# Q and K transposed by the DMA for six of eight batches, with a new order of attention work, loads and early matmuls, in a fused attention and feed-forward kernel

## Chip, cores, metric

One core of a Trainium2 chip. The metric is device time in microseconds (us). One execution of each kernel was also profiled; its span, from first to last instruction, is 1.7 to 1.8 us shorter than the time of that same execution. TensorE is called warm here where its granted clock is full, and cold where it is half.

## The reference, cut

```python
# q, k, v: (8 batches, 12 heads, 448 rows, 64), float32
scores = (1 / sqrt(64)) * q @ k.T
attn   = maximum(scores, 0) ** 2 / 448
x      = (attn @ v), heads side by side          # (3584, 768)
xn     = x / sqrt(mean(x * x, -1) + 1e-6) * rms_g
out    = (silu(xn @ w_gate) * (xn @ w_val)) @ w_out   # d_ff = 1536
```

## The kernel before

All matmuls are bf16. Work is cut into units; for each batch b the units of the feed-forward of b ("main") are merged with the attention units of b+1 ("side"). Each engine runs its own instructions in the order in which the program emits them, so a unit's place decides what stands behind what on every engine.

```python
def head_rows(t, b, h0, h1):                       # 4 rows of a head stand next to each other: 512-byte pieces in bf16
    return t[b, h0:h1].rearrange("h (p c) d -> p h (c d)", c=NCH)      # p = 112, c = 4
...
for s in range(NSL):                               # weights in 4 slices
    load_w("g", s)
    load_w("v", s)
    if s == 1:                                     # Q and K of batch 1 in the middle of the weights
        alloc_ld(1); load("q", 1); load("k", 1)
load("v", 1)
...
def reorder(b, j):                                 # VectorE: bring the two heads of a pair side by side
    for nm in ("q", "k"):
        t = tpool.tile([PC, NCH, 2, D], BF16, ...)
        nc.vector.tensor_copy(out=t (h c reordered), in_=ld[nm, b][:, 2*j : 2*j+2, :])
        ldp[nm, b, j] = t

def transposes(b, j):
    ...                                            # reorder(b, 0) if j == 0; reorder(b, j+1)
    psT = ps_a.tile([P, 2, S], BF16)
    for ti, nm in enumerate(("q", "k")):
        for c in range(NCH):
            nc.tensor.transpose(out=psT[:, ti, c*PC:(c+1)*PC], in_=ldp[nm, b, j][:, c], identity=ident)
    nc.vector.tensor_copy(out=t, in_=psT)          # PSUM to SBUF

def scores(b, j, cs):                              # 2 score buffers in PSUM (psS)
    ...                                            # matmuls into psS, then per chunk:
    relu on ScalarE (every fourth on VectorE); square at once on VectorE

def attention(b):
    units = [transposes(b, 0)]
    for j in range(HP):                            # 6 pairs of heads
        units += [scores(b, j, (0, 1)), transposes(b, j+1), scores(b, j, (2, 3)), attend(b, j-1)]
    units += [attend(b, HP-1)]

def norm(b):                                       # ones-matmul for the sums, sqrt (ACT), then on VectorE:
    nc.vector.reciprocal(out=rstd, in_=rstd)       # 2.95 us
    for kt in range(KT):                           # 6 x 0.61 us
        nc.vector.scalar_tensor_tensor(out=xn[:, kt], in0=xTs[b][:, kt], scalar=g_sb[:, kt], in1=rstd, ...)
...
merge(ffn(b), attention(b+1) + [norm(b+1)], 0.0, 0.1)   # side units spread over the first 90% of the main work
```

## Time and profile before

| | us |
|---|---|
| timed before, median (four timed runs, 547.5 to 551.92) | 548.75 |
| span of the profiled run | 544.9 |
| head: start to first gate matmul of batch 0 | 51.6 |
| first batch (feed-forward 0 with attention 1) | 64.5 |
| next six batches together | 379.0 |
| tail (feed-forward 7 alone) | 49.9 |

The four stretches run from one "first gate matmul of a batch" to the next, read from the timeline of TensorE.

The summary page, with busy time per engine, the tenths of busy time in 40 equal slices, the granted TensorE clock in tenths, and the chain of waits that ended last:

```profile
span 544.9 us, 7394 instructions
...
PE 485.1 (89%) x3024; PEld 236.1 (43%) x3024; DVE 338.6 (62%) x586; ACT 252.3 (46%) x369; POOL 34.4 (6%) x45
...
PE   3774999879999799888999799987999899989996
...
PEclk9976999979999899999999999999999999999999
...
PE 73%; DVE 14%; ACT 8%; issue 2%; DMA 1%; POOL 0%; ACTq 0%; POOLq 0%
PE psV L260 20%; PE psG L260 20%; PE psO L286 14%; PE psAV L207 8%; PE psS L182 8%; DVE xn L249 5%; DVE rstd L246 4%; ACT r L197 4%; PE psT L163 3%; ACT L243 2%; DVE r L198 2%; DVE r L195 1%; ACT rstd L243 1%; DMA kb<-in_k_dram 1%; ACT xT L
```

TensorE (PE) is the limit, but 14% of the chain is VectorE (DVE): there PE stood still. The stretches of the table, with the busy time of each engine (instructions in brackets), the clock, the share of the DMA engines and GB/s:

```profile
core 0: us, PE busy (x) PEld busy (x) DVE busy (x) ACT busy (x) POOL busy (x), PEclk, DMA share, GB/s
0.00:51.59 51.59, 27.48 (x158) 13.25 (x159) 36.43 (x67) 23.38 (x28) 20.42 (x30) 0.85 1.25 179
51.59:116.04 64.45, 59.28 (x369) 28.25 (x367) 42.35 (x73) 29.57 (x44) 2.80 (x3) 0.95 0.73 115
116.04:495.03 378.99, 354.48 (x2263) 171.21 (x2261) 249.63 (x430) 187.34 (x275) 11.19 (x12) 0.99 0.25 44
495.03:544.90 49.87, 43.81 (x242) 23.38 (x239) 10.22 (x17) 12.02 (x22) 0.00 (x0) 1.00 0.14 40
```

In the head VectorE is busy 36 of 52 us and PE only 27; in the six batches PE is busy 354 of 379 us. Tile names below: qp and kp are the reordered Q and K, psT their transposes in PSUM and qkT the copy of them, psS the scores and r their relu, psAV attention times V, psSS the sums for norm, psG and psV the gate and value units, psO the output projection. What PE waited for (total us, times, longest):

```profile
PE psT L163 <- DVE qp L148: 29.6, 8, 7.6
PE psS L182 <- ACT r L197: 7.4, 11, 1.0
PE psS L182 <- DVE r L195: 7.4, 9, 1.1
PE psS L182 <- DVE qkT L169: 4.3, 2, 3.3
```

The largest is the first transposes of a batch, which wait for the reorder copy of Q (tile qp): 4.8 us at the very start, where the copy itself waits for its load, 7.6 at the end of the head, and 2.9 at each of six later boundaries. The timeline of PE and of VectorE at the second boundary (start, duration, instruction, idle before it):

```profile
107.09 5.37 PE L286 MATMUL psO<-wo_sb,hT 128*128 128x256 bf16 x36
115.32 0.56 PE L163 MATMUL psT<-ident,qp 112*128 112x112 bf16 x4 [2.86 <-DVE qp L148]
115.67 0.58 PE L163 MATMUL psT<-ident,kp 112*128 112x112 bf16 x4
116.04 2.45 PE L260 MATMUL psG<-xn,wg_sb 128*128 128x448 bf16 x6
```

```profile
108.41 2.95 DVE L246 RECIPROCAL rstd<-rstd 128x448 f32<-128x448 f32 x1 [1.55 <-ACT rstd L243]
111.40 3.66 DVE L249 SCALAR_TENSOR_TENSOR xn<-xT,g_sb,rstd 128x448 bf16<-128x448 bf16 x6
114.98 0.29 DVE L148 COPY qp<-qb 112x512 bf16<-112x512 bf16 x1
```

PE finishes its output projection at 112.46 and stands until 115.32, because the copy of 0.29 us was emitted after norm and stands behind the reciprocal and six xn. The first gate unit after it is at half clock (2.24 us from start to start where a warm unit takes 1.13).

### The profile page before, as it was taken

What the parts mean: (1) busy time and instruction counts of PE and PEld (TensorE: products, weight loads), DVE (VectorE), ACT (ScalarE), POOL (GpSimd) and SP (SyncE); (2) the same over time, 40 slices, a digit from 0 to 9 for tenths busy, and PEclk for the clock granted to TensorE, in tenths of its full rate; (3) what the DMA queues carried; (4) which work ended last, traced back from release to release, by engine and by line L of the source; (5) the groups of instructions that cost most, each with busy time, mean ns of one, the idle gap of its engine ahead of it and who ended that gap; (6) DMA issues with size and microseconds to landing.
All of it is one profiled execution on the core that took longest, in us unless ns stands there. A gap on an engine that the chain in (4) does not pass through costs nothing.

```text
span 544.9 us, 7394 instructions
## 1 busy us (share of the span) xinstructions
PE 485.1 (89%) x3024; PEld 236.1 (43%) x3024; DVE 338.6 (62%) x586; ACT 252.3 (46%) x369; POOL 34.4 (6%) x45
## 2 busy tenths in 40 slices
PE   3774999879999799888999799987999899989996
PEld 1331444434444344444444444444445444444553
DVE  3886677467764677566774677656775677745210
ACT  2553454524545354535444454454545445553221
POOL 7330001000010001000010000100000000000000
PEclk9976999979999899999999999999999999999999
DMA  9999938150073402560054500733001200002013
GB/s 114 201 201 205 203 53 102 35 103 1 1 102 73 95 1 24 79 123 16 1 75 86 108 1 1 103 58 80 1 1 29 78 10 2 1 29 59 0 30 88
DMA packets 45858, 35.08 MB, mean 64 GB/s; under 512 B 2304, under 2 KB 42240, under 8 KB 45824
## 3 DMA queue, kind: packets, MB, share of 16 engines
q0 software_dynamic: 40560, 23.60, 31.7%
q1 hardware_dynamic: 5264, 11.02, 6.8%
q8 instruction: 23, 0.38, 0.3%
q14 instruction: 11, 0.09, 0.1%
HBM read 47.19 MB, written 11.01 MB: 107 GB/s over the span
## 4 chain that ended last, share of the span: by engine, by line
PE 73%; DVE 14%; ACT 8%; issue 2%; DMA 1%; POOL 0%; ACTq 0%; POOLq 0%
PE psV L260 20%; PE psG L260 20%; PE psO L286 14%; PE psAV L207 8%; PE psS L182 8%; DVE xn L249 5%; DVE rstd L246 4%; ACT r L197 4%; PE psT L163 3%; ACT L243 2%; DVE r L198 2%; DVE r L195 1%; ACT rstd L243 1%; DMA kb<-in_k_dram 1%; ACT xT L215 1%
## 5 line engine op out<-in xcount | busy, mean ns | idle before, releaser
L198 DVE TENSOR_TENSOR r<-r 112x896 bf16<-112x896 bf16 x192 | 119.3, 625 | 93.8 <-ACT r L197 91.9
L197 ACT ACTIVATE r<-psS 112x896 bf16<-112x896 f32 x144 | 127.0, 916 | 52.5 <-PE psS L182 52.4
L260 PE MATMUL psG<-xn,wg_sb 128*128 128x448 bf16 x576 | 129.4, 360 | 1.1 <-DVE xn L249 1.0
L260 PE MATMUL psV<-xn,wv_sb 128*128 128x448 bf16 x576 | 128.0, 359 | 0.0
L286 PE MATMUL psO<-wo_sb,hT 128*128 128x512 bf16 (+1 forms) x672 | 115.2, 326 | 0.0
L271 ACT ACTIVATE sil<-psG 128x448 bf16<-128x448 f32 x96 | 52.3, 545 | 102.2 <-PE psG L260 90.8
L277 DVE TENSOR_TENSOR hT<-sil,psV 128x448 bf16<-128x448 bf16 x96 | 59.4, 618 | 45.9 <-PE psV L260 37.8
L286 PEld LDWEIGHTS <-hT 128*128 128x128 bf16 x672 | 63.6, 98 | 49.2 <-issue 9.3
L182 PE MATMUL psS<-qkT 64*112 64x448 bf16 x384 | 64.5, 394 | 19.3 <-ACT r L197 7.4
L260 PEld LDWEIGHTS <-wg_sb 128*128 128x128 bf16 x576 | 53.0, 99 | 59.8 <-issue 19.2
L260 PEld LDWEIGHTS <-wv_sb 128*128 128x128 bf16 x576 | 52.3, 99 | 57.5 <-issue 19.2
L293 ACT COPY ost<-psO 128x512 f32<-128x512 f32 (+1 forms) x56 | 26.9, 480 | 81.4 <-PE psO L286 81.4
L195 DVE TENSOR_SCALAR r<-psS 112x896 bf16<-112x896 f32 x48 | 52.0, 1084 | 0.0
L207 PE MATMUL psAV<-r,vb 112*64 112x448 bf16 x384 | 47.7, 370 | 4.6 <-DVE qkT L169 3.8
L182 PEld LDWEIGHTS <-qkT 64*112 64x112 bf16 x384 | 21.1, 131 | 60.5 <-issue 55.2
L163 PE MATMUL psT<-ident,qp 112*128 112x112 bf16 x192 | 19.0, 226 | 29.6 <-DVE qp L148 29.6
L215 ACT ACTIVATE xT<-psAV 128x448 bf16<-128x448 f32 x48 | 26.1, 545 | 33.7 <-PE psAV L207 33.7
L163 PEld LDWEIGHTS <-qp 112*128 112x128 bf16 x192 | 14.0, 103 | 40.9 <-DVE qp L148 31.9
L207 PEld LDWEIGHTS <-vb 112*64 112x64 bf16 x384 | 19.1, 111 | 28.9 <-issue 21.4
L246 DVE RECIPROCAL rstd<-rstd 128x448 f32<-128x448 f32 x8 | 23.6, 2953 | 12.8 <-ACT rstd L243 12.8
L169 DVE COPY qkT<-psT 128x896 bf16<-128x896 bf16 x48 | 29.8, 620 | 2.3 <-PE psT L163 2.1
L249 DVE SCALAR_TENSOR_TENSOR xn<-xT,g_sb,rstd 128x448 bf16<-128x448 bf16 x48 | 29.3, 680 | 0.3
(39 smaller groups left out, 157.6 us busy)
## 6 DMA issues: line engine op xcount, KB each, us to landing
qb<-in_q_dram POOLq DMA_DIRECT2D x7, 672.0 KB, 7.3
kb<-in_k_dram POOLq DMA_DIRECT2D x7, 672.0 KB, 9.8
vb<-in_v_dram POOLq DMA_DIRECT2D x7, 672.0 KB, 8.1
out_dram<-ost SPq DMA_DIRECT2D x8, 336.0 KB, 2.8
wg_sb<-in_moe_w_gate_dram POOLq DMA_DIRECT2D x4, 576.0 KB, 20.2
wv_sb<-in_moe_w_val_dram POOLq DMA_DIRECT2D x4, 576.0 KB, 21.8
wo_sb<-in_moe_w_out_dram POOLq DMA_DIRECT2D x2, 1152.0 KB, 28.3
out_dram<-ost SPq DMA_DIRECT2D x8, 288.0 KB, 5.3
```

Of the source, the lines that this page charges most:

```text
L163: nc.tensor.transpose(out=psT[:, ti, c * PC : (c + 1) * PC], in_=ldp[nm, b, j][:, c, :, :], identity=ident[:],)
L182: nc.tensor.matmul(out=psS[:, hh, :S], lhsT=t[prt, 1, c * PC : (c + 1) * PC], rhs=t[prt, 0, :], start=True, stop=True,)
L195: nc.vector.tensor_relu(out=r[:], in_=psS[:, :, :S])
L197: nc.scalar.activation(out=r[:], in_=psS[:, :, :S], func=ACT.Relu)
L198: nc.vector.tensor_tensor(out=r[:], in0=r[:], in1=r[:], op=ALU.mult)
L207: nc.tensor.matmul(out=psAV[hh * D : (hh + 1) * D, :], lhsT=ld["v", b][:, 2 * j + hh, c * D : (c + 1) * D], rhs=rsq[b, j, c][:, hh, :], st ...
L246: nc.vector.reciprocal(out=rstd[:], in_=rstd[:])
L249: nc.vector.scalar_tensor_tensor(out=xn[:, kt, :], in0=xTs[b][:, kt, :], scalar=g_sb[:, kt : kt + 1], in1=rstd[:], op0=ALU.mult, op1=ALU.mult,
L260: nc.tensor.matmul(out=ps[:], lhsT=w_sb[:, kt, fb * P : (fb + 1) * P], rhs=xns[b][:, kt, :], start=(kt == 0), stop=(kt == KT - 1),)
L271: nc.scalar.activation(out=s[:], in_=psG[:], func=ACT.Silu)
L277: nc.vector.tensor_tensor(out=hTs[b // 2][:, fb, o : o + S], in0=sil[b, fb][:], in1=psV[:], op=ALU.mult)
L286: nc.tensor.matmul(out=ps[:, :w], lhsT=hTs[i][:, fk, t * P : (t + 1) * P], rhs=wo_sb[:, fk, o : o + w], start=(fk == 0), stop=(fk == FT - 1),)
```

## The change

Its intent: take transposes off PE and VectorE; keep PE warm and busy at the start; give norm and its VectorE work more matmuls to hide behind. It
- loads Q and K of batches 2 to 7 so that a row of all heads lies in one partition (128-byte pieces instead of 512), and transposes them from SBUF to SBUF with eight DMA transposes per batch, issued by SyncE (SP);
- transposes batches 0 and 1 on PE straight from the loaded layout, one head at a time (16 half-width transposes per pair instead of 8), without reorder copies;
- loads all gate and value weights before Q, K and V of batch 1;
- runs 40 matmuls on zeros in the head;
- defers each square by one unit, joins the second score unit with attend (15 side units instead of 25), and spreads the side work over 85% of the main work instead of 90%;
- in passing, moves three relus of batch 0 from VectorE to ScalarE, gives x one buffer instead of two, and puts the transposes of PE in another PSUM pool.

```diff
+    def transpose_dma(b):
+        new_qkT(b)
+        for ti, nm in enumerate(("q", "k")):
+            for c in range(NCH):
+                nc.sync.dma_start_transpose(
+                    out=qkT[b][:, :, ti, c * PC : (c + 1) * PC], in_=ld[nm, b][:, c, :]
+                )
...
+            nc.gpsimd.dma_start(
+                out=t[:].rearrange("p c (h d) -> p c h d", d=D)[:, :, h0:h1, :],
+                in_=src.rearrange("h (p c) d -> p c h d", c=NCH),
+            )
...
     for s in range(NSL):
         load_w("g", s)
         load_w("v", s)
-        if s == 1:
-            alloc_ld(1)
-            load("q", 1)
-            load("k", 1)
-    load("v", 1)
+    for nm in ("q", "k", "v"):
+        load(nm, 1)
...
-    def reorder(b, j):
...
             for c in range(NCH):
-                nc.tensor.transpose(out=psT[:, ti, ...], in_=ldp[nm, b, j][:, c, :, :], ...)
+                for hh in range(2):
+                    nc.tensor.transpose(out=psT[hh * D : (hh + 1) * D, ti, ...],
+                                        in_=ld[nm, b][:, 2 * j + hh, c * D : (c + 1) * D], ...)
...
+        if b < PE_T:                                  # PE_T = 2
+            add(0.4, lambda: transposes(b, 0))
         for j in range(HP):
...
+            add(1.2, lambda j=j: scores(b, j, (2, 3)), lambda j=j: j and attend(b, j - 1))
...
+    keep_busy(16)
...
+            at = len(main) * 2 // 3
+            main[at:at] = [(0, lambda b=b: transpose_dma(b + 2))]
-        for fn in merge(ffn(b), side, 0.0, 0.1):
+        for fn in merge(main, side, 0.0, 0.15):
```

More of the change, by code (lines that the diff above doesn't have):

```diff
@@ L66 @@
     ldpool = ctx.enter_context(tc.tile_pool(name="ld", bufs=2))
-    tpool = ctx.enter_context(tc.tile_pool(name="tsb", bufs=2))
+    qtpool = ctx.enter_context(tc.tile_pool(name="qkT", bufs=2))
     apool = ctx.enter_context(tc.tile_pool(name="attn", bufs=10))
-    xpool = ctx.enter_context(tc.tile_pool(name="xT", bufs=2))
+    xpool = ctx.enter_context(tc.tile_pool(name="xT", bufs=1))
     npool = ctx.enter_context(tc.tile_pool(name="norm", bufs=2))
@@ L76, with new_qkT @@
     ps_m = ctx.enter_context(tc.tile_pool(name="ps_m", bufs=3, space=bass.MemoryType.PSUM))
-    def head_rows(t, b, h0, h1):
-        return t[b, h0:h1].rearrange("h (p c) d -> p h (c d)", c=NCH)
     ld = {}
-    def alloc_ld(b):
-        for nm in ("q", "k", "v"):
-            ld[nm, b] = ldpool.tile([PC, H, NCH * D], BF16, name=nm + "b", tag=nm + "b")
+    qkT = {}
+    src_of = {"q": q, "k": k, "v": v}
+    PE_T = 2
     def load(nm, b, h0=0, h1=H):
-        src = {"q": q, "k": k, "v": v}[nm]
-        nc.gpsimd.dma_start(out=ld[nm, b][:, h0:h1, :], in_=head_rows(src, b, h0, h1))
+        runs = nm == "v" or b < PE_T
+        if (nm, b) not in ld:
+            shape = [PC, H, NCH * D] if runs else [PC, NCH, H * D]
+            ld[nm, b] = ldpool.tile(shape, BF16, name=nm + "b", tag=nm + "b")
+        t = ld[nm, b]
+        src = src_of[nm][b, h0:h1]
+        if runs:
+            nc.gpsimd.dma_start(out=t[:, h0:h1, :], in_=src.rearrange("h (p c) d -> p h (c d)", c=NCH))
+        else:
+            nc.gpsimd.dma_start(
+                out=t[:].rearrange("p c (h d) -> p c h d", d=D)[:, :, h0:h1, :],
+                in_=src.rearrange("h (p c) d -> p c h d", c=NCH),
+            )
+    def new_qkT(b):
+        qkT[b] = qtpool.tile([P, HP, 2, S], BF16, name="qkT", tag="qkT")
+    def transpose_dma(b):
[5 more added lines that the diff above has]
+                )
     wg_sb = wpool.tile([P, KT, F], BF16, name="wg_sb", tag="wg")
@@ L110, in load_wo, with keep_busy @@
         )
-    alloc_ld(0)
+    ones_bf = const.tile([P, P], BF16, name="ones_bf", tag="ones_bf")
+    nc.vector.memset(ones_bf[:], 1.0)
+    busy_bf = const.tile([P, S], BF16, name="busy_bf", tag="busy_bf")
+    nc.vector.memset(busy_bf[:], 0.0)
+    def keep_busy(n):
+        ps = ps_m.tile([P, S], FP32, name="psB", tag="mm")
+        for _ in range(n):
+            nc.tensor.matmul(out=ps[:], lhsT=ones_bf[:], rhs=busy_bf[:], start=True, stop=True)
     load("q", 0, 0, 2)
@@ L116 @@
     masks.make_identity(nc, ident[:])
-    ones_bf = const.tile([P, P], BF16, name="ones_bf", tag="ones_bf")
-    nc.vector.memset(ones_bf[:], 1.0)
     eps_col = const.tile([P, 1], FP32, name="eps_col", tag="eps_col")
@@ L141, with relu_on, square_on, flush @@
     xTs = {}
-    qkT = {}
-    ldp = {}
-    def reorder(b, j):
-        for nm in ("q", "k"):
-            t = tpool.tile([PC, NCH, 2, D], BF16, name=nm + "p", tag=nm + "p")
-            nc.vector.tensor_copy(
-                out=t[:].rearrange("p c h d -> p h c d"),
-                in_=ld[nm, b][:, 2 * j : 2 * j + 2, :].rearrange("p h (c d) -> p h c d", c=NCH),
-            )
-            ldp[nm, b, j] = t
     def transposes(b, j):
         if j == 0:
-            xTs[b] = xpool.tile([P, KT, S], BF16, name="xT", tag="xT")
-            reorder(b, 0)
-        if j + 1 < HP:
-            reorder(b, j + 1)
-        psT = ps_a.tile([P, 2, S], BF16, name="psT", tag="ps_a")
+            new_qkT(b)
+        psT = ps_m.tile([P, 2, S], BF16, name="psT", tag="mm")
         for ti, nm in enumerate(("q", "k")):
             for c in range(NCH):
-                nc.tensor.transpose(
-                    out=psT[:, ti, c * PC : (c + 1) * PC],
-                    in_=ldp[nm, b, j][:, c, :, :],
-                    identity=ident[:],
-                )
-        t = tpool.tile([P, 2, S], BF16, name="qkT", tag="qkT")
-        nc.vector.tensor_copy(out=t[:], in_=psT[:])
-        qkT[b, j] = t
-    rsq = {}
-    state = {"n": 0}
+                for hh in range(2):
+                    nc.tensor.transpose(
+                        out=psT[hh * D : (hh + 1) * D, ti, c * PC : (c + 1) * PC],
+                        in_=ld[nm, b][:, 2 * j + hh, c * D : (c + 1) * D],
+                        identity=ident[:],
+                    )
+        nc.vector.tensor_copy(out=qkT[b][:, j, :, :], in_=psT[:])
+    rsq = {}
+    pending = []
+    def relu_on(b, j, c):
+        return "dve" if c == 3 and (b or j % 2) else "act"
+    def square_on(b, j, c):
+        return "dve"
+    def flush():
+        while pending:
+            pending.pop(0)()
     def scores(b, j, cs):
-        t = qkT[b, j]
         pss = []
@@ L183, in scores @@
                     out=psS[:, hh, :S],
-                    lhsT=t[prt, 1, c * PC : (c + 1) * PC],
-                    rhs=t[prt, 0, :],
+                    lhsT=qkT[b][prt, j, 1, c * PC : (c + 1) * PC],
+                    rhs=qkT[b][prt, j, 0, :],
                     start=True,
@@ L189, in scores @@
             pss.append(psS)
+        squares = []
         for c, psS in zip(cs, pss):
             r = apool.tile([PC, 2, S], BF16, name="r", tag="r")
-            on_dve = state["n"] % 4 == 3
-            state["n"] += 1
-            if on_dve:
+            if relu_on(b, j, c) == "dve":
                 nc.vector.tensor_relu(out=r[:], in_=psS[:, :, :S])
@@ L197, in scores @@
                 nc.scalar.activation(out=r[:], in_=psS[:, :, :S], func=ACT.Relu)
-            nc.vector.tensor_tensor(out=r[:], in0=r[:], in1=r[:], op=ALU.mult)
+            eng = nc.gpsimd if square_on(b, j, c) == "pool" else nc.vector
+            squares.append(
+                lambda r=r, eng=eng: eng.tensor_tensor(out=r[:], in0=r[:], in1=r[:], op=ALU.mult)
+            )
             rsq[b, j, c] = r
+        flush()
+        pending.extend(squares)
     x2s = {}
@@ L213, in attend, with add @@
                 )
+        if j == 0:
+            xTs[b] = xpool.tile([P, KT, S], BF16, name="xT", tag="xT")
+            x2s[b] = npool.tile([P, KT, S], BF16, name="x2", tag="x2", bufs=1)
         xT = xTs[b]
         nc.scalar.mul(out=xT[:, j, :], in_=psAV[:], mul=inv_attn)
-        if j == 0:
-            x2s[b] = npool.tile([P, KT, S], BF16, name="x2", tag="x2")
-        nc.vector.tensor_tensor(out=x2s[b][:, j, :], in0=xT[:, j, :], in1=xT[:, j, :], op=ALU.mult)
-    def attention(b):
-        units = [(0.4, lambda: transposes(b, 0))]
-        for j in range(HP):
-            units.append((0.5, lambda j=j: scores(b, j, (0, 1))))
-            if j + 1 < HP:
-                units.append((0.4, lambda j=j: transposes(b, j + 1)))
-            units.append((0.5, lambda j=j: scores(b, j, (2, 3))))
-            if j:
-                units.append((0.8, lambda j=j: attend(b, j - 1)))
-        units.append((0.8, lambda: attend(b, HP - 1)))
+        pending.append(
+            lambda: nc.vector.tensor_tensor(
+                out=x2s[b][:, j, :], in0=xT[:, j, :], in1=xT[:, j, :], op=ALU.mult
+            )
+        )
+    def attention(b):
+        units = []
+        def add(cost, *fns):
+            units.append((cost, lambda: [f() for f in fns]))
+        if b < PE_T:
+            add(0.4, lambda: transposes(b, 0))
+        for j in range(HP):
+            add(0.5, lambda j=j: scores(b, j, (0, 1)))
+            if b < PE_T and j + 1 < HP:
+                add(0.4, lambda j=j: transposes(b, j + 1))
+            if b == 0:
+                add(0.3, lambda: keep_busy(2))
+            add(1.2, lambda j=j: scores(b, j, (2, 3)), lambda j=j: j and attend(b, j - 1))
+            if b == 0:
+                add(0.3, lambda: keep_busy(2))
+        add(0.1, flush)
+        add(0.8, lambda: attend(b, HP - 1), flush)
         return units
@@ L321 @@
             side = attention(b + 1) + [(1.1, lambda b=b: norm(b + 1))]
+        main = ffn(b)
         if b + 2 < B:
-            alloc_ld(b + 2)
             for nm in ("q", "k", "v"):
                 load(nm, b + 2)
-        for fn in merge(ffn(b), side, 0.0, 0.1):
+            at = len(main) * 2 // 3
+            main[at:at] = [(0, lambda b=b: transpose_dma(b + 2))]
+        for fn in merge(main, side, 0.0, 0.15):
             fn()
```

## The prediction

> **What bounds the kernel now.** TensorE. The summary gives PE 89% busy, DVE 62%, ACT 46%; the chain of waits is 73% PE. By the timeline: a head of 51 us (attention of batch 0, norm), seven batches of 58.6 to 67.3 us (feed-forward of b merged with attention of b+1), a tail of 50 us.
> - Head: VectorE-bound (17.5 of 20 us busy from 20 to 40 us). Per head pair: 4 squares (0.62), a relu (1.08), two reorder copies (0.29), a PSUM copy (0.62), x2 (0.39): 5.1 us, the measured period.
> - Boundaries: in the view of waits, PE's transposes wait 29.6 us for the reorder copy of Q, which stands behind the reciprocal (2.95) and six xn (3.66): 7.6 us in the head, 2.9 later. After the first two, the clock halves for two gate/value units (2.24 us, not 1.13).
> - Inside a batch: transposes 0.40 us per pair, waits for score buffers 1 to 2.4 us per batch, and units beside attention pieces take 1.24, not 1.13.
>
> **What changes, costed.**
> 1. Batches 2 to 7: no PE transposes, -2.4 us each; VectorE -7 us each, off the path.
> 2. A batch now opens with scores, needing no VectorE, and norm moves from 0.86 to 0.79 of the main work: 8 to 9 us of matmuls cover the 8 us after the norm's sums. -3 us per boundary and before the tail; about -4 for clock dips.
> 3. 15 side pieces instead of 25: about -1 us per batch.
> 4. Head: VectorE falls to 4.0 us per pair, ACT 3.8; I take 4.5. First scores 2.5 us earlier. Keep-busy matmuls (about 10 us) fill idle PE time. 51 to about 44.
> 5. Batches 0, 1: 16 half-width transposes per pair instead of 8, +0.1 to 0.4 us per pair.
> 6. Q and K of 2 to 7 land in 128-byte instead of 512-byte pieces, four times the packets. A full queue now spends about 48 ns per 512-byte packet; I estimate 30 to 60 per small one: 10 to 20 us per load (7 to 10 now). The Trainium skill, "DMA: Bandwidth & Descriptors", Specifications, says transfers below 512 B cost a read-modify-write; no trace here shows it yet. Loads can run a batch ahead, so this hides, except for batch 2, queued behind all weights (about 57 us).
> 7. Eight DMA transposes of 168 KB per batch, issued at two thirds of the previous batch: 19 us until needed. The skill's figures disagree: "VectorE: DVE Perf Modes", The three transpose paths: 1309 ns per 128x128, an estimated 55 us per batch if serial; the DMA page's 261 GB/s: about 5 us plus latency. No trace here shows one. I take 10 to 20.
>
> **Sum.** Head 44, first batch 60, six batches 341 (now 380), tail 47: span 492, plus 2.6 by which timed runs exceed the span; with something for new waits, 500 us. Range 484 to 522. Faster 0.84, within 2% 0.09, slower 0.07.
>
> **What would show it.** PE transposes gone after batch 1; PE waits for xn or Q copies near zero at boundaries; batches of about 55 to 58 us; first gate unit at 44 us; DMA transposes landing in under 19 us.
>
> **What would make it wrong.** Transposes over 19 us: scores wait at each boundary, 6 times the excess. Q and K of batch 2 landing after 85 us: one wait of 5 to 15 us. Small packets filling the DMA, delaying everything. ACT or the two score buffers becoming the limit.

## More of the kernel before

"Median" is the median of a kernel's timed executions.

In the six batches the clock is half from 116.04 to 121.45 and from 182.89 to 186.30 us, and full otherwise: 8.8 us at half clock, which cost an estimated 4.4.

## The result and the profile after

The changed kernel takes 487.23 us (four runs, 487.0 to 487.78); the ratio to before is 0.8873, 95% interval 0.8829 to 0.8916. The time lies inside the predicted range.

| stretch, us | before | predicted | after |
|---|---|---|---|
| head | 51.6 | 44 | 48.6 |
| first batch | 64.5 | 60 | 58.6 |
| six batches | 379.0 | 341 | 330.1 |
| tail | 49.9 | 47 | 48.0 |
| span | 544.9 | 492 | 485.3 |

The summary page of the changed kernel:

```profile
span 485.3 us, 7083 instructions
...
PE 459.0 (95%) x2856; PEld 220.2 (45%) x2872; DVE 284.2 (59%) x452; ACT 253.8 (52%) x372; POOL 50.8 (10%) x45
...
PE   7960999999999999999999999999999999999995
...
PEclk9995899999999999999999999999999999999999
...
PE 86%; DMA 8%; POOL 1%; DVE 1%; ACT 1%; issue 1%; POOLq 0%
PE psG L295 24%; PE psV L295 23%; PE psO L321 21%; PE psS L199 9%; PE psAV L228 8%; DMA kb<-in_k_dram 5%; DMA wv_sb<-in_moe_w_val_dram 3%; PE psSS L273 1%; DVE xn L284 1%; PE psT L173 1%; DVE rstd L281 1%; POOL kb L93 0%; POOL qb L93 0%; AC
```

PE's share of the chain rose from 73 to 86%, and VectorE's fell from 14 to 1%: the largest share beside PE is 8% of DMA. The stretches, same columns as before:

```profile
0.00:48.62 48.62, 29.55 (x254) 12.52 (x255) 28.69 (x49) 25.26 (x31) 22.42 (x30) 0.89 1.26 179
48.62:107.17 58.55, 58.28 (x402) 27.41 (x403) 36.19 (x58) 29.11 (x45) 10.78 (x6) 0.97 1.63 153
107.17:437.29 330.12, 328.25 (x1967) 156.89 (x1978) 211.57 (x335) 187.41 (x275) 17.57 (x10) 1.00 0.57 72
437.29:485.30 48.01, 42.90 (x240) 23.37 (x239) 7.72 (x13) 12.02 (x22) 0.00 (x0) 1.00 0.15 42
```

In the six batches PE is now busy 328 of 330 us. Its busy time fell by 26 us, its idle time by another 23. What PE waits for:

```profile
PE psT L173 <- DMA qb<-in_q_dram: 10.2, 1, 10.2
PE psT L173 <- DMA kb<-in_k_dram: 3.6, 2, 2.9
PE psS L199 <- ACT r L213: 2.6, 8, 0.4
PE psB L139 <- DVE eps_col L146: 1.3, 1, 1.3
PE psG L295 <- DVE xn L284: 0.9, 4, 0.2
```

The waits for reorder copies are gone. The largest wait left is a new one in the head: 10.2 us for the load of Q of batch 1, and 2.9 more for its K. A boundary now (compare the four lines of before):

```profile
266.85 7.96 PE L321 MATMUL psO<-wo_sb,hT 128*128 128x512 bf16 x47
274.75 0.59 PE L199 MATMUL psS<-qkT 64*112 64x448 bf16 x4
275.26 1.31 PE L295 MATMUL psG<-xn,wg_sb 128*128 128x448 bf16 x6
```

Scores, whose operands now come from the DMA, start at once; the first gate unit follows without a wait for xn, at full clock. Only the first of these boundaries (107.17 us) still waits for xn: the 0.9 us of the list.

To see where the six batches gained, I took all starts of PE's groups of matmuls from the timeline, counted the time from each start to the next under the first group's tile, and set apart what the timeline marks as a wait (so short pacing below its limit stays with the tile):

| us in the six batches | before | after |
|---|---|---|
| transposes (psT) | 14.0 | 0 |
| waits of transposes for reorder copies | 14.3 | 0 |
| waits for score buffers (psS) | 10.2 | 0 |
| score matmuls (psS) | 40.4 | 36.7 |
| gate, value, output, norm sums (psG, psV, psO, psSS) | 268.4 | 260.2 |
| attend (psAV) | 31.7 | 31.9 |
| waits for xn, and other | 0 | 1.4 |
| sum | 379.0 | 330.1 |

So less than a third of the gain in these batches is the transposing itself. The rest is waits, and slower units. This table cannot tell matmuls at half clock from changeovers to and from the attention pieces, but the clock can: half clock cost about 4.4 us before (above) and nothing after, where the clock is full in all six batches. That leaves some 7.5 of the 11.9 us by which units and scores fell; the changeovers are a likely reason, not a shown one.

### The profile page after: what moved, and what is told of

The parts are those of the page before. It is cut to its first block, busy times and chain, and to the rows that moved or that the text cites. A ratio compares the mean times of both kernels' runs of the same rounds, so it can differ in the third digit from the quotient of the medians.

```text
span 485.3 us, 7083 instructions
## 1 busy us (share of the span) xinstructions
PE 459.0 (95%) x2856; PEld 220.2 (45%) x2872; DVE 284.2 (59%) x452; ACT 253.8 (52%) x372; POOL 50.8 (10%) x45
## 4 chain that ended last, share of the span: by engine, by line
PE 86%; DMA 8%; POOL 1%; DVE 1%; ACT 1%; issue 1%; POOLq 0%
PE psG L295 24%; PE psV L295 23%; PE psO L321 21%; PE psS L199 9%; PE psAV L228 8%; DMA kb<-in_k_dram 5%; DMA wv_sb<-in_moe_w_val_dram 3%; PE psSS L273 1%; DVE xn L284 1%; PE psT L173 1%; DVE rstd L281 1%; POOL kb L93 0%; POOL qb L93 0%; ACT r L213 0%; POOL vb L93 0%
## 5 line engine op out<-in xcount | busy, mean ns | idle before, releaser
L295 PE MATMUL psG<-xn,wg_sb 128*128 128x448 bf16 x576 | 127.0, 356 | 0.9 <-DVE xn L284 0.9
L295 PE MATMUL psV<-xn,wv_sb 128*128 128x448 bf16 x576 | 125.4, 354 | 0.0
L321 PE MATMUL psO<-wo_sb,hT 128*128 128x256 bf16 (+1 forms) x656 | 111.5, 325 | 1.2 <-issue 0.5
L216 DVE TENSOR_TENSOR r<-r 112x896 bf16<-112x896 bf16 x192 | 110.0, 618 | 0.3 <-ACT r L213 0.2
L199 PE MATMUL psS<-qkT 64*112 64x448 bf16 x384 | 57.6, 372 | 3.3 <-ACT r L213 2.6
L211 DVE TENSOR_SCALAR r<-psS 112x896 bf16<-112x896 f32 x45 | 48.9, 1088 | 17.4 <-PE psS L199 17.4
L199 PEld LDWEIGHTS <-qkT 64*112 64x112 bf16 x384 | 18.0, 124 | 39.1 <-issue 36.3
L93 POOL DMA_DIRECT2D vb<-in_v_dram x9 | 8.1, 903 | 211.0 <-PE psAV L228 156.6
L95 POOL DMA_DIRECT2D qb<-in_q_dram x6 | 13.8, 2306 | 35.5 <-DMA qkT<-kb 32.7
L178 DVE COPY qkT<-psT 128x896 bf16<-128x896 bf16 x12 | 7.5, 621 | 15.7 <-PE psT L173 15.7
## 6 DMA issues: line engine op xcount, KB each, us to landing
qb<-in_q_dram POOLq DMA_DIRECT2D x7, 672.0 KB, 14.2
kb<-in_k_dram POOLq DMA_DIRECT2D x7, 672.0 KB, 22.5
```

The costliest lines, as they stand in the source:

```text
L199: nc.tensor.matmul(out=psS[:, hh, :S], lhsT=qkT[b][prt, j, 1, c * PC : (c + 1) * PC], rhs=qkT[b][prt, j, 0, :], start=True, stop=True,)
L211: nc.vector.tensor_relu(out=r[:], in_=psS[:, :, :S])
L216: lambda r=r, eng=eng: eng.tensor_tensor(out=r[:], in0=r[:], in1=r[:], op=ALU.mult)
L295: nc.tensor.matmul(out=ps[:], lhsT=w_sb[:, kt, fb * P : (fb + 1) * P], rhs=xns[b][:, kt, :], start=(kt == 0), stop=(kt == KT - 1),)
L321: nc.tensor.matmul(out=ps[:, :w], lhsT=hTs[i][:, fk, t * P : (t + 1) * P], rhs=wo_sb[:, fk, o : o + w], start=(fk == 0), stop=(fk == FT - 1),)
```

## The experiments

Main theory: the gain is a sum of separate savings on PE, each readable from the trace. The rivals are named in each expectation. All kernels of the experiments are correct except the one made wrong. Lines of the kernel differ a little between variants, so L-numbers are not comparable; tiles are.

**1. The kernel before without reorder copies** (`e7_before_direct`): 

```diff
-            reorder(b, 0)
-        if j + 1 < HP:
-            reorder(b, j + 1)
...
-                nc.tensor.transpose(out=psT[:, ti, ...], in_=ldp[nm, b, j][:, c, :, :], ...)
+                for hh in range(2):
+                    nc.tensor.transpose(out=psT[hh * D : (hh + 1) * D, ti, ...],
+                                        in_=ld[nm, b][:, 2 * j + hh, c * D : (c + 1) * D], ...)
```

> The kernel before with only the reorder copies removed: PE transposes each head straight from the loaded layout, 16 instead of 8 per pair. Theory A: PE's transposes no longer stand behind xn in VectorE's order, but the first gate still does, so each of 8 boundaries gives about 2.3 us and the head 3, against 0.1 us x 48 more transposing: about 530 us. Rival H (the boundary wait was set by the norm chain, whoever is first to wait for it): 545 us or more.

Measured: 535.31 us, ratio 0.9768 (0.974 to 0.9796): 5 us above theory A, 10 below the rival. The wait moved, shortened, from the transposes to the first gate:

```profile
PE psG L258 <- DVE xn L247: 9.3, 23, 3.9
PE psS L180 <- ACT r L195: 8.9, 14, 1.0
PE psS L180 <- DVE r L193: 7.4, 9, 1.1
```

Taking the copies out of VectorE's queue is worth 13 us even though the chain of norm stays: a gate unit can start on the first xn, while the copy had to wait for the last. Not all of it is boundaries between batches: of the 10.7 us by which the profiled span is shorter, 5.3 are in the head, 1.3 in the first batch and 4.2 in the six batches, where the longer transposes took back 4.1. The waits for score buffers in the six batches stayed (10.1 us). The 16 half-width transposes cost PE 0.50 us per pair instead of 0.39 (psT 18.1 and 14.0 us in the six batches).

**2. The kernel before with only the spread changed** (`e11_before_spread15`):

```diff
-        for fn in merge(ffn(b), side, 0.0, 0.1):
+        for fn in merge(ffn(b), side, 0.0, 0.15):
```

> The kernel before with only the spread of the side work changed from 90% to 85%. Theory A: norm is issued about 2 us earlier in each batch, which shortens the wait for the reorder copies behind xn from 2.9 to about 0.9 us at six boundaries and removes the wait before the tail; with the clock dips about 15 us: 533 us. If the place of norm mattered only once the reorder copies are gone: 546 us or more.

Measured: 534.14 us, ratio 0.9764 (0.9711 to 0.9816). The number is as expected: one constant is worth 14 us (the interval reaches past 0.98, so that it is faster is clear, but not that it is so by 2%). The mechanism is only half as expected: the wait of transposes in the six batches fell from 14.3 to 7.5 us, but the waits for score buffers, which the theory did not name, fell as much, from 10.2 to 2.7; new short waits of attend took 2.8. The waits for the copies over the whole span (29.6 before):

```profile
PE psT L163 <- DVE qp L148: 23.2, 8, 7.6
```

**3. Only the new transposes, old schedule** (`e5_dma_only_old_schedule`): the changed kernel with the old list of units, squares at once, the old load order, the relus of batch 0 as before, no keep-busy matmuls (x keeps its one buffer and the transposes their new pool), and

```diff
-        for fn in merge(main, side, 0.0, 0.15):
+        for fn in merge(main, side, 0.0, 0.1):
```

> The kernel before plus only the new transposes (DMA for batches 2 to 7, per head on PE for 0 and 1, no reorder copies): old unit list, old spread, squares at once, old load order, no keep-busy matmuls. Theory A: saves 14 us of PE transposes, about 2 us at each of 7 boundaries, 4 of clock dips and 3 in the head: about 513 us. Rival B: 495 us or less.

Measured: 505.09 us, ratio 0.9194 (0.9161 to 0.9226): 8 us below the main theory, 10 above the rival. The theory had left out that the waits for score buffers would go with the transposes (0.5 us left in the six batches of 10.2). Added to the old schedule, then, the new transposes, with the reorder copies gone, take off 43 of the 61 us; taken out of the new one the DMA transposes are worth less (experiments 4 and 5). The parts of the change remove some of the same waits, so their worths do not add up.

**4. Everything but the DMA transposes** (`e1_pe_transposes_all`):

```diff
-    PE_T = 2
+    PE_T = 8
```

(and the DMA transposes only for b + 2 >= PE_T, so never).

> The changed kernel with PE transposes per head for all eight batches and no DMA transposes; everything else of the change kept. Theory A (the gain is the sum of several separate savings on TensorE): only the PE time comes back. A pair of heads costs 16 transposes, 0.44 us in two groups of 0.22 plus about 0.08 of switching, 0.52 us x 6 pairs x 6 batches = 19 us, so about 506 us, boundaries still free of waits. Rival B (the DMA transposes carry most of the 61 us): 530 us or more.

Measured: 520.56 us, ratio 0.9486 (0.9449 to 0.9522), between the two. Against the changed kernel, the six batches hold 31.4 us more: 18.0 of transposes, 4.7 of waits for score buffers, 1.9 of waits for xn, 3.6 in gate units, 2.0 in score matmuls, 1.2 in the rest. The main theory named only the first. With transposes the side list has 21 units instead of 15 (the expectations say 20), and norm, its last, is emitted later.

**5. The same with the side work spread over 80%** (`e12_pe_all_spread20`):

```diff
-        for fn in merge(main, side, 0.0, 0.15):
+        for fn in merge(main, side, 0.0, 0.2):
```

> The run with PE transposes for all batches (520.6 us, 33 more than the changed kernel, of which the transposes themselves explain 18), with the side work spread over 80% of the main work instead of 85%. Theory L (20 side pieces instead of 15 put norm later, so the first gate at three of six boundaries is paced by xn; that is 5 to 6 of the missing 15 us): about 514 us. Rival M (the rest is only score-buffer waits and switching on PE): 520 us.

Measured: 510.59 us, ratio 0.9318 (0.9282 to 0.9354): 10 us less, more than expected. In the six batches the waits for xn (2.8 before) and for score buffers (4.7 before) are both gone from the account. So against a schedule tuned for it, the DMA transposes are worth about 23 us (510.6 - 487.2), not 33; most of that is the 18 us of transposing. The changed kernel itself was not tried with a spread of 80%.

**6. Norm late again** (`e3_norm_late`):

```diff
-        for fn in merge(main, side, 0.0, 0.15):
+        for fn in merge(main, side, 0.0, 0.1):
```

> The changed kernel with the side work spread over 90% of the main work as before, instead of 85%. Theory A: norm then has about 6.5 us of matmuls behind it against a chain of 8 us, so PE waits 1.0 to 1.3 us for xn at each of 7 boundaries: about 495 us. Rival D (the old boundary waits came only from the reorder copies in VectorE's order, not from where norm stands): 488 us.

Measured: 497.67 us, ratio 0.9063 (0.903 to 0.9097): 10 us more than the changed kernel, so the place of norm matters with the copies gone too.

```profile
PE psG L295 <- DVE xn L284: 6.5, 28, 0.2
```

28 waits of at most 0.25 us are one first gate unit after another, paced by the xn multiplications. The unit takes 2.7 us instead of 1.14.

**7. DMA transposes later in SP's order** (`e9_transposes_last`):

```diff
-            at = len(main) * 2 // 3
+            at = len(main)
```

> The changed kernel with the eight DMA transposes of a batch placed after the last unit of the previous batch instead of at two thirds of it. On the queue of SP they then stand behind that batch's last output store. Theory J (what decides when they run is their place among SP's own instructions; at two thirds they run at the start of the batch, 15 us for eight with about 40 us to spare): now they start at the boundary and scores wait about 14 us at each of 6 boundaries, plus cold matmuls after it: 570 to 590 us. Rival K (they run as soon as their data and buffer are there, wherever they stand): 487 us.

Measured: 578.0 us, ratio 1.0545 (1.049 to 1.06). Slower than before the change, from one moved line. In the changed kernel, SP's own order has the transposes of batch b+2 right after the stores of batch b-1; SP at that time (first line: stores, then four transposes of Q and three of the four of K, up to the end of the window):

```profile
209.50 9.72 SPq L335 DMA_DIRECT2D out_dram<-ost  x6
219.33 7.16 SPq L107 DMA_TRANSPOSE qkT<-qb  x4
226.59 6.50 SPq L107 DMA_TRANSPOSE qkT<-kb  x3
```

They run at the start of the batch and are read only after the next boundary, at 274.75. In the experiment they stand behind the last stores of the batch, which wait for the output:

```profile
248.01 4.68 SPq L335 DMA_DIRECT2D out_dram<-ost  x4
252.81 5.21 SPq L107 DMA_TRANSPOSE qkT<-qb  x4
258.12 5.22 SPq L107 DMA_TRANSPOSE qkT<-kb  x4
```

```profile
PE psS L199 <- DMA qkT<-kb: 72.0, 16, 9.8
```

and scores at 260.89 wait 9.4 us, with cold matmuls after it (granted clock 0.916 in the mean, 0.986 in the changed kernel). Of the 91 us more, 72.0 are these waits. It was not data that was late: every load of Q and K issued before had landed by 208.1 us, and the waits of SP show only stores waiting for their output. The Trainium skill, "DMA: Bandwidth & Descriptors", Anatomy of one DMA, says that DMA engines do not wait on semaphores and that any wait happens on the issuing sequencer before dispatch. This trace agrees: the first transpose is issued at 252.81, just after the last store of the batch (whose issue ended at 252.69), and not before.

**8. Squares at once** (`e6_squares_at_once`):

```diff
-            squares.append(lambda r=r, eng=eng: eng.tensor_tensor(out=r[:], in0=r[:], in1=r[:], op=ALU.mult))
...
-        flush()
-        pending.extend(squares)
+            nc.vector.tensor_tensor(out=r[:], in0=r[:], in1=r[:], op=ALU.mult)
```

(likewise the squares of x for norm).

> The changed kernel with each square issued right after its relu instead of one unit later. Theory F (deferring the squares lets VectorE's relu free the score buffers sooner, and that is why the 10 us of waits for score buffers in six batches went): 492 to 497 us, with PE waiting for the scores' buffers again. Rival G (those waits went with the copies that VectorE no longer does): within 1 us of 487, or 1 to 3 us more from the head alone.

Measured: 492.44 us, ratio 0.8982 (0.8956 to 0.9008). The number is in theory F's range, its mechanism is not: in the six batches waits for score buffers came back by 1.1 us only, of 10.2, and the six batches lost 2.0 us; 2.0 more were lost in the first batch, where VectorE still copies transposes. The deferral is worth about 5 us by the timed runs, 4 by the spans; it is not why those 10 us went. Rival G does not stand either: experiment 1 took the reorder copies off VectorE and kept 10.1 of these 10.2 us. What removed them was not isolated: the spread alone left 2.7 (experiment 2), the DMA transposes under the old spread 0.5 (experiment 3), and the new schedule with PE transposes none (experiment 5). Several parts of the change do it, each without the others.

**9. Large pieces, wrong** (`e8_wide_pieces_wrong`):

```diff
-                out=t[:].rearrange("p c (h d) -> p c h d", d=D)[:, :, h0:h1, :],
-                in_=src.rearrange("h (p c) d -> p c h d", c=NCH),
+                out=t[:].rearrange("p c (g e) -> p (c g) e", e=NCH * D),
+                in_=src.rearrange("h (p c) d -> p h (c d)", c=NCH),
```

> The changed kernel with Q and K of batches 2 to 7 loaded in 512-byte pieces into the same tile, so that the DMA transposes find the wrong order: wrong result on purpose, same bytes, a quarter of the packets. Theory A (loads run ahead, small pieces are hidden): 487 us within 1. Rival I (the small pieces and their contention cost time now, in the first batches above all): 484 us or less.

Measured: 486.8 us, ratio 0.8883 (0.8855 to 0.8911): the same. The queue of the loads, in the changed kernel and here (packets, MB, share of 16 engines' span):

```profile
q0 software_dynamic: 88944, 23.60, 50.5%
```

```profile
q0 software_dynamic: 40560, 23.60, 35.3%
```

The loads take half the DMA's time instead of a third, and all of the rise is hidden.

**10. Q and K of batch 1 early** (`e2_q1k1_early`):

```diff
         load_w("g", s)
         load_w("v", s)
-    for nm in ("q", "k", "v"):
-        load(nm, 1)
+        if s == 1:
+            load("q", 1)
+            load("k", 1)
+    load("v", 1)
```

> The changed kernel with Q and K of batch 1 loaded after the second of four weight slices, as before the change, instead of after all weights. Theory A: the 10.2 + 2.9 us that PE waits for these two loads go; the first gate is then paced by xn, ready 39 to 42 us instead of 48.6, so about 7 us less: 480 us. Rival C (the loading is full to 70 us either way, so the wait only moves to weight slices or to Q and K of batch 2): 486 us or more.

Measured: 480.13 us, ratio 0.8741 (0.8714 to 0.8769): 7 us less than the changed kernel, as expected. The first gate matmul comes at 40.2 instead of 48.6 us; the first batch gives 2.4 us back.

```profile
35.13 0.39 PE L175 MATMUL psT<-ident,qb 112*64 112x112 bf16 x8
37.58 0.39 PE L175 MATMUL psT<-ident,kb 112*64 112x112 bf16 x8 [2.07 <-DMA kb<-in_k_dram]
40.17 0.35 PE L297 MATMUL psG<-xn,wg_sb 128*128 128x448 bf16 x1 [2.20 <-DVE xn L286]
```

Here PE waits 2.07 us for K and 2.20 for xn, where it waited 10.2 and 2.9 for the loads. "All weights first" was the one part of the change that cost time.

**11. The same without keep-busy matmuls** (`e4_q1k1_early_no_busy`): all three calls of keep_busy taken out of experiment 10.

```diff
-    keep_busy(16)
...
-            if b == 0:
-                add(0.3, lambda: keep_busy(2))
```

> The version with Q and K of batch 1 loaded early (480.1 us), without the 40 keep-busy matmuls of the head. Theory A: with the load wait gone the head is paced by ACT and VectorE at 3.9 us per pair of heads; at half clock the pair's own PE work (scores 1.9, attend 1.7, transposes 0.8) is 4.4 us and takes over, so 2 to 3 us more: about 482.5. Rival E (PE is idle for half of the head, so its clock does not matter): 480 or a little less.

Measured: 481.28 us, ratio 0.8791 (0.8765 to 0.8816), against 0.8741 (0.8714 to 0.8769) with them. The intervals touch, the two ran in different calls, and the profiled spans are 478.9 without and 479.1 with, the first gate at 40.24 and 40.17 us. Inconclusive about one microsecond; the 2 to 3 us of theory A are not there.

**12. An attempt at the fastest version** (`e10_early_and_spread`), on experiment 10:

```diff
-        if s == 1:
+        if s == 0:
...
-        for fn in merge(main, side, 0.0, 0.15):
+        for fn in merge(main, side, 0.0, 0.15 if b else 0.2):
```

> An attempt at the fastest version: Q and K of batch 1 loaded after the first weight slice, and the side work of the first batch alone spread over 80% of the main work, because its 20 side pieces put norm too late for the first boundary (first gate paced by xn, 1.6 us over the others). Theory A: 1.5 us from the boundary and 0 to 1 us from the 2.1 us that PE waits for K: about 478 us. Otherwise 480.1, as the early version alone.

Measured: 478.48 us, ratio 0.8735 (0.8703 to 0.8766). It is the fastest of all; its lead over experiment 10 (480.13) is within the intervals of the ratios, but the trace shows the step: the batch after the first boundary takes 56.81 us instead of 58.36.

## Why the prediction was right, point by point

It foretold 500 us, in a range of 484 to 522; 487.2 came. Predicted savings of 48.75 us are 79% of the 61.5 measured. The span that it added up (492) was nearer than the figure it gave (500).

- *PE bounds the kernel, and its transposes go* (point 1): right. 14.0 us of transposing went in six batches, 2.4 each were foretold.
- *Boundaries* (point 2): right in mechanism, and in size but for the tail. 14.3 us of waits for copies in the six batches became 0.9 of waits for xn; before the tail 1.9 us went, not 3. Experiments 1, 2 and 6 show two causes apart: what stands in VectorE's order before PE's first need, and where norm is emitted. Each alone gave 13 to 14 us from before, but not all of that at the boundaries: half of the first is in the head, and half of the second is waits for score buffers.
- *Clock dips and side pieces* (points 2 and 3): about 10 us foretold; gate, value, output, norm sums and scores together fell by 11.9 us (308.8 to 296.9). Right in size. By the clock about 4.4 of it are the dips (4 foretold); that the other 7.5 are the fewer side pieces (6 foretold) was not tested.
- *Score buffers*: the missing term. The prediction listed 1 to 2.4 us of such waits per batch among what bounds the kernel and credited nothing for them, and even added time "for new waits". They were 10.2 us in six batches and all went. The six batches came out 11 us below the 341 foretold, which is about this term; the other terms of the six batches came out near their size.
- *Head, 51 to about 44* (point 4): the mis-sized term, 48.6 came. VectorE's part came out better than foretold: a pair of heads took 3.9 us, not 4.5, and the end of the head's attention, where norm's sums start, moved from 41.0 to 32.9 us. But the prediction has no term for the load of Q and K of batch 1, which the change put behind all gate and value weights: PE got K at 48.1 us, 6 us after the last xn (42.2). Experiment 10 gives 40.2 when they come early. The keep-busy matmuls, which were to fill idle time, brought about a microsecond, if anything (experiment 11, with the early load). The two misses, 5 us here and 11 in the six batches, have opposite signs; that they partly cancel in the sum is luck.
- *Half-width transposes* (point 5): right, 0.11 us more per pair.
- *Small pieces* (point 6): right that they hide (experiment 9). Loads of Q landed after 14.2 us (median), in the range of 10 to 20; those of K after 22.5, above it. Between the two queue lines of experiment 9, 48384 more packets took 15.2% of 16 engines for 486 us more, about 1180 us. Before, 31.7% of 16 engines for 544.9 us over 40560 packets make 68 ns each, so the 16128 packets of Q and K that were replaced took some 1100 us, and the 64512 in their place 2280: an estimate of 35 ns per small packet. 30 to 60 had been taken. The Trainium skill, "DMA: Bandwidth & Descriptors", Specifications, warns of a read-modify-write below 512 B; no run here separates that from the shorter transfer, and no time of the kernel hangs on it.
- *DMA transposes* (point 7): their duration was right: issuing eight took 12 to 15 us, and the last landed 13 to 19 us after the first issue, in a range of 10 to 20. The premise "issued at two thirds of the previous batch: 19 us until needed" was wrong. SP does not run at PE's pace: they were issued at the start of the batch and had about 55 us (219.3 to 274.75). That they hide was foretold for a wrong reason: with 19 us, the slowest batch (19.1) would have had nothing to spare. Experiment 7 shows what the place in SP's order is worth, 91 us.

## What to carry to other kernels

Read each engine's instruction stream as a queue of its own: a 0.29 us copy behind a 6.6 us chain, or a DMA behind a store that is not ready, costs what stands in front of it; one moved line was worth 91 us in experiment 7. When operations move to an idle engine, retune the schedule on both sides before saying what the move was worth: here the DMA transposes looked like 43 us when added to the old schedule (with the reorder copies gone), 33 when taken out of the new one, and 23 when that was then tuned for PE transposes (the side with DMA transposes was not tuned again). After a saving in the first stage, look at which load is now late there; "weights first" cost 7 us because the next batch's inputs were needed earlier.

## What the Trainium skill lacked or had wrong

- Duration of DMA transposes. "VectorE: DVE Perf Modes", The three transpose paths, gives 1309 ns for 128x128, an estimated 55 us for our eight (each 112x768, 5.25 such blocks) if run one after the other; "DMA: Bandwidth & Descriptors", Latency and other measured facts, gives 261 GB/s, an estimated 5 us for 1.38 MB. Eight issued back to back from SBUF to SBUF took 10.4 us of issue time beside little other traffic (5.21 + 5.22 in experiment 7), landing 2.7 us after issue (median), and 15 us beside loads, landing after 2.8 to 8.8 (the batch at 219.3 us of the changed kernel). Neither figure serves here; 1.3 us of issue per 172 KB transpose does, with the landing added.
- "DMA: Bandwidth & Descriptors" names the wait on the issuing sequencer, but no page draws the scheduling consequence, that a DMA transpose stands behind earlier stores of its issuing engine, or gives a price: here 487 against 578 us for one moved line.
- "TensorE: Matmul & The Clock Gate", Part 4, gives about 275 to 390 ns as the duration of a transpose of 128x128, and lacks the pitch in a stream. One of 112x128 took 212 ns (median) in the kernel before, and four of them started within 0.20 us when warm, an estimated 50 ns each; 16 half-width ones took 0.50 us per pair of heads.
- The same page, Part 1, puts the return to half clock after at least one idle window of about 3.4 us. In the kernel before, waits of 2.86 us were followed by half clock at two boundaries and by full clock at four. At the first of the two the clock fell at 114.62, when PE had stood for only 2.16 us (the last columns are clock, DMA share and GB/s; ends of matmuls are modelled), so a wait somewhat below the window is not safe:

```profile
112.46:114.62 2.16, 0.00 (x1) 0.00 (x0) 2.16 (x5) 0.37 (x1) 0.00 (x0) 1.00 0.92 277
114.62:115.32 0.70, 0.00 (x0) 0.00 (x1) 0.70 (x3) 0.00 (x0) 0.00 (x0) 0.50 0.66 228
```
